# Attention and top-1 routing in one kernel: expert 2's w1 issued behind expert 0's late rows, some routing steps moved in slots 31 to 35, and expert 1's w2 cast by VectorE

## The chip, the cores and the metric

The kernel runs on one core of a Trainium2 chip. The metric is the device time of one execution, in microseconds (us). The time before is 264.27 us, the median of three executions (263.95, 264.27, 265.75). Each kernel also has one profiled execution, from which all the views below come.

## What is computed

The first half is a linear attention for 8 batches of 8 heads, with 576 tokens and 64 channels a head, followed by a norm over each head's channels. The second half takes the result as 4608 tokens of 512 channels, sends each token to one of 8 experts, and runs a two-layer network there.

```python
kv  = einsum('bhsd,bhse->bhde', k, v)
out = einsum('bhsd,bhde->bhse', q, kv)
x   = out / sqrt(mean(out*out, -1) + 1e-6) * g_norm      # then (4608, 512)

logits = x @ w_gate                                       # (4608, 8)
e      = argmax(logits); gate = softmax(logits)[e]
y[mask of expert e] = gate * (relu(xe @ w1[e]) @ w2[e])   # w1: 512x1024, w2: 1024x512
```

## The kernel before

**Attention in 36 slots.** Each of the 36 slots makes 128 rows of x. In slot s PE multiplies the transposed q with the batch's kv (`x_mm`, L334) into a PSUM tile, ACT squares it and VectorE (DVE) adds the squares up (`x_norm`, L348, lines 361 and 365), ACT takes a logarithm and an exponential for the inverse norm, and DVE writes the small logits (L373) and the scaled rows in f16 (L381). PE also transposes the q of two slots ahead (`x_qt`), and ACT copies it out of PSUM (`x_qs`). From slot 31 on the scaling of a slot is held over into the next one.

**Routing.** A `Route` (L396) treats a group of two to five slots: sum the logits, take their maximum (`top`), subtract it (`below`, which gives dl), mark the first maximum (`code`, `first`, `choose`), count with a scan (`tally`), exponentials (`expo`, L467, on ACT), ranks within each expert by three small matmuls of PE (`ranks`, L457, which write into spare columns of a slot's PSUM tile), then the row numbers (`mask`, `send`) and the running total (`total`), all on DVE. `scatter` (L488) is an indirect DMA of GpSimd that writes 128 rows of x, sorted by expert, into a scratch tensor in DRAM (`xs_scratch`). The last three groups are slots 27 to 30, 31 to 33, and 34 to 35.

**Order by hand.** The order on every engine's queue is that of the program text. The slot loop runs lists of closures: `mid` after `x_mm` of the slot, `pre`, `head`, `late` and `last` after it. `at(where, s, fn)` puts a step into one of them, and the table `plan` (L907) gives each group's slots. [...]

**Weights.** A weight matrix is loaded in f32 (2 MB) into one of five staging buffers that it shares with q, k and v (`load_next`, L196: w1 and w2 of expert 0, then of expert 1, and so on), and cast to f16: w1 by DVE (`cast1`, L177) or ACT (`cast1_act`, L183), w2 by ACT (`cast2`, L188), or by DVE where an engine is named (L190).

**Experts.** `fetch` (L664) is a transposing DMA on SP of an expert's rows out of the scratch tensor into xt, with the marks mt (token numbers and gates) in a DMA of their own. It must wait until the scatters in question have landed. The first 384 rows of expert 0 (NE = 3 tiles) and 256 of expert 1 (NA = 2 tiles) are fetched after slot 30, the late rest when the last scatters have landed. `early_one`, `early_pair`, `ahead_pair` and `late_pair` are the first layer on these parts (tiles hpe, hpa, hpl), with a ReLU on ACT into xh; `two` (L782) is the second layer of 128 rows (ype, yp), DVE scales the result (L805) and GpSimd writes it to the output by an indirect DMA (L808).

**After the slots** the text of L1073 to L1137 interleaves the two last groups' routing with the first matmuls of experts 0 and 1; the loop of L1143 then runs the experts: `one` (first layer, four PSUM buffers hp), the casts of the next expert's w1, the loads of w2 three experts ahead and the rows of that expert, `two` for each tile with the casts of the next expert's w2 between them on ACT, and the next w1.

Of the kernel before, what the change touches and what calls it, by code (L numbers as in the profile page):

```python
# [21 lines left out]
def _bc(ap: bass.AP, insert_pos: int, count: int) -> bass.AP:  # L22
    dims = [list(d) for d in ap.ap]
    dims.insert(insert_pos, [0, count])
    return bass.AP(tensor=ap.tensor, offset=ap.offset, ap=dims)
# [3 lines left out]
def kernel(  # L29
# [11 lines left out]
    nc = tc.nc  # L41
# [150 lines left out]
    W = [Weights(e, e) for e in range(E)]  # L192
# [3 lines left out]
    def load_next(count=1):  # L196
        nonlocal n_loads
        for _ in range(count):
            if n_loads < len(loads):
                n, m = loads[n_loads]  # L200
                (W[n].load1 if m == 1 else W[n].load2)(stg[n_loads % 5], nc.sync)
                n_loads += 1
# [93 lines left out]
    def split(s):  # L296
        P, r = divmod(s, 9)
        b = 2 * P + (r >= 4)
        return P, r, b
# [34 lines left out]
    def x_mm(s):  # L334
        P, r, b = split(s)
        if r < 8:
            parts = [(slice(0, 128), kvs_bufs[b % 4])]
        else:
            parts = [(HALF[tok], kvs_bufs[(2 * P + tok) % 4]) for tok in range(2)]
        ops[s] = quad("kvp" if s in (32, 35) else "op", "op")  # L340
        for i4 in range(4):
            for cols, kvs in parts:
                nc.tensor.matmul(  # L343
                    ops[s][cols, i4, 0:144], qts[s][:, i4, cols], kvs[:, i4, :],
                    start=True, stop=True,
                )

    def x_norm(s):  # L348
        P, r, b = split(s)
        if r == 0:  # L350
            xgs[P] = xh[P % 2][:, 0:9 * RW].rearrange("p (g c) -> p g c", g=9)
            lrs[P] = PW.tile([128, 9, 8, 8], F32, tag="lr", bufs=2, name="lr")
        if r == (2, 2, 2, 3)[P]:
            nc.gpsimd.tensor_copy(
                xgs[P][:, :, 512:514].bitcast(I32).rearrange("p g o -> p (g o)"),
                tokc[:, 9 * P:9 * P + 9],
            )
        xg, lr = xgs[P], lrs[P]
        oc = ops[s]
        sq = PW.tile([128, 8, 64], F32, tag="sq", bufs=1, name="sq")  # L360
        nc.scalar.activation(  # L361
            sq.rearrange("p (c i) n -> p c (i n)", i=2), oc[:, :, 0:128], ACTF.Square
        )
        ms = PW.tile([128, 8], F32, tag="ms", bufs=3, name="ms")
        nc.vector.reduce_sum(ms, sq, axis=AXX)  # L365

        def scale():
            lnt = PW.tile([128, 8], F32, tag="lnt", bufs=3, name="lnt")
            nc.scalar.activation(lnt, ms, ACTF.Ln, scale=1.0 / 64.0, bias=epsb)
            rinv = PW.tile([128, 8], F32, tag="rinv", bufs=3, name="rinv")  # L370
            nc.scalar.activation(rinv, lnt, ACTF.Exp, scale=-0.5)  # L371
            r2 = rinv.rearrange("p (c i) -> p c i", i=2)
            nc.vector.tensor_tensor(  # L373
                lr[:, r, :, :].rearrange("p (c i) n -> p c i n", i=2),
                oc[:, :, 128:144].rearrange("p c (i n) -> p c i n", i=2),
                _bc(r2, 3, 8), op=ALU.mult,
            )
            return r2

        def rows(r2):  # L380
            nc.vector.tensor_tensor(  # L381
                xg[:, r, 0:512].rearrange("p (i c n) -> p c i n", i=2, c=4),
                oc[:, :, 0:128].rearrange("p c (i n) -> p c i n", i=2),
                _bc(r2, 3, 64), op=ALU.mult,
            )

        def rest():
            r2 = scale()
            return lambda: rows(r2)

        return rest
# [473 lines left out]
    with tc.tile_pool(name="psattn", bufs=1, space=bass.MemoryType.PSUM) as PSA:  # L865
        first_slot = [9 * (b // 2) + 4 * (b % 2) for b in range(B)]
        mid, pre, head, late, last = ({s: [] for s in range(-4, 40)} for _ in range(5))
# [15 lines left out]
        def at(where, s, fn, *args):  # L883
            where[s].append(lambda: fn(*args))

        for b in range(1, B):
# [24 lines left out]
            ((1, 5, 4), (18, 19, 20, 21), (22, 23, 24, 25)),  # L911
            ((2, 0, 5), (23, 24, 25, 26), (26, 27, 28, 28, 29)),
            ((2, 5, 4), (27, 28, 28, 29), (29, 29, 30, 30)),
            ((3, 0, 4), (31, 31, 31, 32), (32, 33, 33, 34)),
        ]
        for g, (s_sum, s_below, s_oh, s_rank), s_scat in plan:
            rt, G = Route(*g), g[2]
            at(late, s_sum, rt.logits, 0, G)
            at(late, s_below - (s_below == s_oh > s_sum), rt.top)
            at(late, s_below, rt.below)  # L920
            at(late, s_below, rt.code)
            at(late, s_oh, rt.expo)
            at(late, s_oh, rt.first)
            at(late, s_oh, rt.choose)
            at(late, s_oh, rt.tally)
            at(late if s_rank == 32 else mid, s_rank, rt.ranks, s_rank)
            at(late, s_rank, rt.mask)
            at(late, s_rank, rt.send)
            at(late, s_rank + (g[0] < 2), rt.total)
            for t, slot in enumerate(s_scat):  # L930
                at(late, slot, rt.scatter, t, t + 1)
        at(last, 2, load_all, ("k", 4), ("v", 4))
# [10 lines left out]
        at(late, 30, lambda: early_close(ecp[0]))  # L943
        at(last, 30, jobs[0].fetch, 0, NE)
        at(last, 30, jobs[1].fetch, 0, NA)
        at(last, 32, load_next, 1)
        for m in range(8):
            at(last if m < 4 else late, 27 + m, W[0].cast1_act, m)
        for n in range(31, 35):
# [1 line left out]
        rt = Route(3, 4, 3)  # L951
        at(late, 34, rt.logits, 0, 3)
        at(late, 34, rt.top)
        at(late, 34, rt.below)
        at(late, 34, rt.expo)
        at(late, 34, rt.code)
        at(late, 34, rt.first)
        at(late, 34, rt.choose)
# [115 lines left out]
        job.hidden()  # L1074
        x_mm(35)
        rest = x_norm(35)
        relu = [job.early_one(0, "qtp"), job.early_one(1, "misc")]
        rt.ranks(34)
        rt.mask()
# [40 lines left out]
            if t < 2:  # L1120
                W[1].cast1(2 * t)
        jobs[1].fetch(NA, CT)
        load_next(1)
        jobs[2].fetch()
        load_next(1)
        jobs[1].hidden()
# [1 line left out]
        for n, tag in enumerate(tags):  # L1128
            jobs[1].ahead_pair(2 * n, tag)
        jobs[1].place(0, NA, evalid[:, NE:NE + NA], ebig[:, NE:NE + NA])  # L1130
        for m in range(2):
            W[1].cast2(m)
        for n, tag in enumerate(tags):
            job.late_pair(2 * n, tag)
        for m in range(2, 4):
            W[1].cast2(m)
        job.place(NE, CT)  # L1137

    PSF = ctx.enter_context(
# [89 lines left out]
```

## Time and profile before

| | us |
|---|---|
| median of three executions | 264.27 |
| profiled execution | 263.74 |
| span in its profile | 261.9 |
| PE busy | 240.9 (92%) |
| ACT busy | 155.1 (59%) |
| DVE busy | 141.8 (54%) |
| GpSimd busy | 101.7 (39%) |

The span is the time from the first to the last instruction in the profile; the profiled execution's own time has 1.8 us around it. In the profile, PE is TensorE's matmuls, PEld its weight loads, POOL GpSimd, and a name such as SPq is an engine's instruction queue. An entry like `hp<-xt,w1b` names the tile written and the tiles read. The page also gives the DMA totals: 83.13 MB were moved, 317 GB/s in the mean over the span, and 16 weight matrices of 2048 KB were loaded with a median of 13.3 us from issue to landing. The slots run to about 117 us, the interleaved part to about 136, the expert loop to 257.

### The profile page before, as it was taken

How to read it: one execution, taken by the hardware profiler on the slowest of the kernel's cores; microseconds unless marked ns; L12 is line 12 of the kernel's file. 1: busy time of each engine (PE TensorE's matmuls, PEld its weight loads, DVE VectorE, ACT ScalarE, POOL GpSimd, SP SyncE). 2: the span in 40 equal slices, each digit the busy share in tenths (PEclk: the TensorE clock that was granted, in tenths of full speed). 3: DMA queues.
4: the chain of work that ended last, by engine and by line, in shares of the span. 5: the costliest groups of instructions: out<-in, count | busy, mean ns of one | idle time of the engine just before them, and what ended most of it. 6: DMA issues, size and time to landing. Idle time of an engine off the chain costs nothing. (4 is left out here: it accounts for less than half of the span.)

```text
span 261.9 us, 7015 instructions
## 1 busy us (share of the span) xinstructions
PE 240.9 (92%) x2786; PEld 173.2 (66%) x2786; DVE 141.8 (54%) x378; ACT 155.1 (59%) x352; POOL 101.7 (39%) x131
## 2 busy tenths in 40 slices
PE   6899978989999997688989999999999999999991
PEld 6778857878879887564566466475674755746640
DVE  0105566868787787869706860488344255156041
ACT  1056747577677779678595738377375547814600
POOL 4032222776278367455602150521504215034063
PEclk9589999999999999989999999999999999999998
DMA  7999999999999999689599996999999999995023
GB/s 227 386 392 390 392 409 382 395 396 394 392 387 404 410 409 398 263 174 371 167 272 327 392 364 118 317 413 239 353 417 216 390 336 295 350 336 216 1 88 120
DMA packets 52106, 83.13 MB, mean 317 GB/s; under 512 B 27862, under 2 KB 27990, under 8 KB 51944
## 3 DMA queue, kind: packets, MB, share of 16 engines
q1 hardware_dynamic: 46900, 68.28, 77.6%
q0 software_dynamic: 4848, 14.20, 14.4%
q10 hardware_dynamic: 324, 0.19, 0.6%
q8 instruction: 22, 0.36, 0.6%
q14 instruction: 12, 0.10, 0.1%
HBM read 63.42 MB, written 16.17 MB: 304 GB/s over the span
## 5 line engine op out<-in xcount | busy, mean ns | idle before, releaser
L808 POOL DMA_INDIRECT out_dram<-ys,idx x41 | 40.4, 985 | 92.3 <-DVE ys L805 84.3
L743 ACT ACTIVATE xh<-hp 128x304 f16<-128x304 f32 (+2 forms) x104 | 44.9, 431 | 38.2 <-PE hp L731 26.2
L797 PE MATMUL yp<-w2b,xh 128*128 128x512 f16 (+1 forms) x296 | 65.4, 379 | 1.2 <-ACT xh L778 1.2
L731 PEld LDWEIGHTS <-w1b 128*128 128x128 f16 x512 | 49.9, 98 | 19.6 <-issue 1.7
L797 PEld LDWEIGHTS <-xh 128*128 128x128 f16 (+1 forms) x320 | 32.5, 102 | 36.3 <-issue 1.2
L731 PE MATMUL hp<-xt,w1b 128*128 128x304 f16 (+2 forms) x416 | 56.4, 296 | 0.0
L805 DVE TENSOR_SCALAR ys<-yp,gate 128x512 f32<-128x512 f32 (+2 forms) x38 | 27.9, 739 | 50.8 <-PE yp L797 50.8
L343 PE MATMUL op<-kvs,qts 128*128 128x144 f32 (+1 forms) x320 | 44.9, 299 | 0.6 <-ACT kvs L291 0.6
L491 POOL DMA_INDIRECT xs_scratch<-xh,sli x36 | 35.5, 987 | 24.2 <-issue 9.5
L343 PEld LDWEIGHTS op<-kvs,qts 128*128 128x128 f32 (+1 forms) x320 | 37.9, 182 | 3.9 <-issue 0.9
L365 DVE TENSOR_REDUCE ms<-sq 128x8 f32<-128x512 f32 x36 | 24.6, 684 | 21.0 <-ACT sq L361 20.3
L310 POOL COPY qp<-land 128x512 f32<-128x512 f32 x32 | 19.5, 616 | 36.1 <-DMA land<-in_q_dram 25.6
L361 ACT ACTIVATE sq<-op 128x512 f32<-128x512 f32 x36 | 21.4, 595 | 14.8 <-PE op L343 11.1
L188 ACT CAST w2b<-land 128x1024 f16<-128x1024 f32 x26 | 25.5, 1045 | 7.1 <-DMA land<-in_moe_w_dram 7.1
L252 PE MATMUL kvp<-land 64*64 64x64 f32 x1152 | 25.6, 234 | 2.7 <-DMA land<-in_v_dram 2.0
L252 PEld LDWEIGHTS kvp<-land 64*64 64x64 f32 x1152 | 21.4, 143 | 7.5 <-issue 7.0
L320 PE MATMUL qtp<-ident,qp 128*128 128x128 f32 x144 | 22.9, 280 | 2.6 <-issue 2.5
L177 DVE TENSOR_SCALAR w1b<-land,g 128x1024 f16<-128x1024 f32 x26 | 18.0, 749 | 12.5 <-DMA land<-in_moe_w_dram 12.5
L381 DVE TENSOR_TENSOR xh<-op,rinv 128x512 f16<-128x512 f32 x36 | 24.5, 679 | 0.3 <-PE op L465 0.3
L326 ACT COPY qts<-qtp 128x512 f32<-128x512 f32 x36 | 21.0, 583 | 4.0 <-PE qtp L320 3.9
L320 PEld LDWEIGHTS qtp<-ident,qp 128*128 128x128 f32 x144 | 17.0, 143 | 3.4 <-issue 3.2
L373 DVE TENSOR_TENSOR lr<-op,rinv 128x64 f32<-128x64 f32 x36 | 7.9, 220 | 12.7 <-ACT rinv L371 9.9
(134 smaller groups left out, 172.9 us busy)
## 6 DMA issues: line engine op xcount, KB each, us to landing
land<-in_moe_w_dram SPq DMA_DIRECT2D x16, 2048.0 KB, 13.3
land<-in_q_dram SPq DMA_DIRECT2D x8, 1152.0 KB, 15.0
land<-in_k_dram SPq DMA_DIRECT2D x7, 1152.0 KB, 15.9
land<-in_v_dram SPq DMA_DIRECT2D x7, 1152.0 KB, 18.9
land<-in_k_dram SPq DMA_DIRECT2D x2, 576.0 KB, 7.2
land<-in_v_dram SPq DMA_DIRECT2D x2, 576.0 KB, 6.3
xs_scratch<-c_zero SPq DMA_DIRECT2D x1, 774.0 KB
out_dram<-ys,idx POOLq DMA_INDIRECT x41, 6.8
```

Source lines behind the costliest of these rows:

```text
L188: nc.scalar.copy(self.w2[:, part, :], self.s2[:, part, :])
L252: nc.tensor.matmul(kvst[b][HALF[ipar], hh, Dh * ip:Dh * ip + Dh], kb[HALF[hh], i, cols], vb[HALF[hh], i, cols], start=(j == 0), stop=(j == 8),
L320: nc.tensor.transpose(qtps[s][:, ip, :, tok, :], qps[s][:, tok, 2 * ip:2 * ip + 2, :], ident)
L343: nc.tensor.matmul(ops[s][cols, i4, 0:144], qts[s][:, i4, cols], kvs[:, i4, :], start=True, stop=True,)
L365: nc.vector.reduce_sum(ms, sq, axis=AXX)
L381: nc.vector.tensor_tensor(xg[:, r, 0:512].rearrange("p (i c n) -> p c i n", i=2, c=4), oc[:, :, 0:128].rearrange("p c (i n) -> p c i n", i=2),
L491: go = nc.gpsimd.indirect_dma_start(out=xs_views[9 * self.P + g0 + t], out_offset=IndirectOffsetOnAxis(ap=self.sli[:, t:t + 1], axis=0), i ...
L731: nc.tensor.matmul(hp, self.w.w1[:, 2 * (kk % 2) + kk // 2, f // 2 * 256:f // 2 * 256 + 256] .rearrange("p (m r) -> p r m", r=2)[:, f % 2, :],
L743: nc.scalar.activation(self.ht[:, f, c0:c1], hp, ACTF.Relu)
L797: nc.tensor.matmul(yp[0:m, :], self.ht[:, f, t * 128:t * 128 + m], self.w.w2[:, f, :], start=(f == 0), stop=(f == 7),)
L805: nc.vector.tensor_scalar(ys[0:m, 0:d], yp[0:m, 0:d], self.gate[0:m, t:t + 1], None, op0=ALU.mult)
L808: nc.gpsimd.indirect_dma_start(out=view, out_offset=IndirectOffsetOnAxis(ap=self.idx[0:m, t:t + 1], axis=0), in_=ys[0:m, 0:d], in_offset=None,
```

## The change

The change has four parts; the number of loads, scatters, casts and matmuls stays the same.

1. The group of slots 27 to 30 has its exponent one slot later (32 instead of 31), and its ranks, mask, row numbers and total move from the end of slot 32 to slot 33, just after that slot's products. The ranks still use slot 32's PSUM tile. All four of its scatters stand in slot 33 (before: one in 32, two in 33, one in 34).
2. The group of slots 31 to 33 has its exponent after slot 35's norm instead of in slot 34.
3. The load of expert 2's w1, which stood at the end of slot 32, is issued after the fetch of the late rows of experts 0 and 1, ahead of expert 2's w2.
4. The four casts of expert 1's w2 are made by DVE, after the first places of expert 1, instead of by ACT in two pairs around the late pairs' ReLUs.

```diff
-            ((3, 0, 4), (31, 31, 31, 32), (32, 33, 33, 34)),
+            ((3, 0, 4), (31, 31, 31, 33), (33, 33, 33, 33)),
...
-            at(late, s_oh, rt.expo)
+            at(late, s_oh + (s_rank == 33), rt.expo)
...
-            at(late if s_rank == 32 else mid, s_rank, rt.ranks, s_rank)
-            at(late, s_rank, rt.mask)
-            at(late, s_rank, rt.send)
-            at(late, s_rank + (g[0] < 2), rt.total)
+            then = mid if s_rank == 33 else late
+            at(mid, s_rank, rt.ranks, min(s_rank, 32))
+            at(then, s_rank, rt.mask)
+            at(then, s_rank, rt.send)
+            at(then, s_rank + (g[0] < 2), rt.total)
...
-        at(last, 32, load_next, 1)
...
-        at(late, 34, rt.expo)
...
         x_mm(35)
         rest = x_norm(35)
+        rt.expo()
...
         jobs[1].fetch(NA, CT)
-        load_next(1)
+        load_next(2)
         jobs[2].fetch()
         load_next(1)
...
-        for m in range(2):
-            W[1].cast2(m)
+        for m in range(4):
+            W[1].cast2(m, nc.vector)
         for n, tag in enumerate(tags):
             job.late_pair(2 * n, tag)
-        for m in range(2, 4):
-            W[1].cast2(m)
         job.place(NE, CT)
```

## The prediction

> **What bounds the kernel now.** I first read the shares of busy time on the page: PE is busy 92% of the span, so the question is where it still waits. The timeline of PE from 100 to 262 us has only three gaps over 0.5 us after slot 31:
>
> ```profile
> 109.06 0.18 PE L461 MATMUL op<-csum,ones 128*128 128x32 f16 x1 [1.97 <-ACT sq L361]
> 116.53 1.46 PE L731 MATMUL hpe<-xt,w1b 128*128 128x384 f16 x8 [0.72 <-DMA xt<-xs_scratch]
> 136.56 3.61 PE L797 MATMUL yp<-w2b,xh 128*128 128x512 f16 x16 [1.25 <-ACT xh L778]
> ```
>
> The square brackets give the idle time before a piece and what ended it. From 136.56 to the last matmul at 256.5 PE never stops: any shift of PE before that goes to the end, unless something else comes late first. What could come late is seen in the timelines of ACT and DVE over the expert loop:
>
> ```profile
> 180.30 3.88 ACT L188 CAST w2b<-land 128x1024 f16<-128x1024 f32 x4 [1.09 <-DMA land<-in_moe_w_dram]
> 198.66 3.88 ACT L188 CAST w2b<-land 128x1024 f16<-128x1024 f32 x4 [2.48 <-DMA land<-in_moe_w_dram]
> 216.59 3.89 ACT L188 CAST w2b<-land 128x1024 f16<-128x1024 f32 x4 [3.52 <-DMA land<-in_moe_w_dram]
> 221.80 8.18 ACT L743 ACTIVATE xh<-hp 128x304 f16<-128x304 f32 x16 [1.32 <-PE hp L731]
> ...
> 190.99 2.74 DVE L177 TENSOR_SCALAR w1b<-land,g 128x1024 f16<-128x1024 f32 x4 [2.45 <-DMA land<-in_moe_w_dram]
> 209.91 2.74 DVE L177 TENSOR_SCALAR w1b<-land,g 128x1024 f16<-128x1024 f32 x4 [4.48 <-DMA land<-in_moe_w_dram]
> 227.89 2.74 DVE L177 TENSOR_SCALAR w1b<-land,g 128x1024 f16<-128x1024 f32 x4 [5.55 <-DMA land<-in_moe_w_dram]
> ```
>
> The reader is to see that the casts wait for their weights, and wait longer with every expert. PE takes 16.9 us an expert (starts of the hp groups: 204.12, 221.02); the loads need some 18 (below). The stock of loaded weights shrinks by about a microsecond an expert, and the last cast of expert 6's w2 ends at 220.48, only 1.32 us before ACT's first ReLU of that expert. The DMA queue is a second bound, just under PE.
>
> Its own order is in the timeline of SP (start, time at the queue, issue):
>
> ```profile
> 115.60 0.42 SPq L165 DMA_DIRECT2D land<-in_moe_w_dram  x1
> 127.68 1.25 SPq L675 DMA_TRANSPOSE xt<-xs_scratch  x1
> ...
> 132.09 0.82 SPq L171 DMA_DIRECT2D land<-in_moe_w_dram  x1
> ...
> 164.48 16.05 SPq L675 DMA_TRANSPOSE xt<-xs_scratch  x1
> 180.77 0.39 SPq L165 DMA_DIRECT2D land<-in_moe_w_dram  x1
> ...
> 200.94 15.81 SPq L675 DMA_TRANSPOSE xt<-xs_scratch  x1
> 216.99 0.39 SPq L165 DMA_DIRECT2D land<-in_moe_w_dram  x1
> ```
>
> 115.60 is expert 2's w1, 132.09 its w2. From there each expert's transposing load holds SP for 16 us behind the two weight loads, and the next weights are issued at once when it ends: issues at 180.77, 199.01, 216.99 are 18.1 us apart. The stages show the same:
>
> ```profile
> 110.00:112.00 2.00, 2.00 (x11) 1.84 (x11) 1.12 (x6) 1.34 (x4) 0.35 (x1) 0.54 0.04 14
> 122.00:124.00 2.00, 2.00 (x14) 1.12 (x13) 1.91 (x7) 2.00 (x3) 1.52 (x2) 1.00 1.04 427
> 126.00:128.00 2.00, 2.00 (x11) 0.88 (x9) 2.00 (x4) 0.72 (x2) 1.14 (x1) 1.00 0.19 66
> 136.00:138.00 2.00, 1.44 (x7) 0.68 (x7) 0.00 (x0) 2.00 (x4) 0.00 (x0) 1.00 1.00 389
> ```
>
> The last three columns are granted PE clock, DMA share and GB/s. DMA is full at 122 to 124 with expert 2's w1, nearly empty at 126 to 128, and full from 130 to 238 but for some 2.5 us at 161 to 164.
>
> [...] The trace agrees: after the 1.97 us gap the granted clock was 0.5 from 110.25 to 113.66. It also shows that a gap of 1.25 us, at 135.3, brings no dip[...]. [...] SP agrees: at 115.60 it has issued the next load, and then nothing for 12 us, until expert 0's late rows may be read (127.68). So a load placed behind that one cannot use the empty queue ahead of it. [...]
>
> **The change, part by part.**
>
> *Ranks, masks and the first exponent (slots 31 to 33).* ACT waits 1.37 us at 107.69 with the exponent for DVE's dl; behind it are a cast (0.70) and the square of slot 32 (108.44 to 109.01), on which PE's ranks wait: the 1.97 us gap. With the exponent a slot later the square ends near 107.4, and with the ranks after slot 33's products PE has 1.8 us of work (zeros 0.6, products 1.2) until the tally (done at 108.72). The gap goes, and with it the dip: the four pieces from 109.58 to 114.08 took 1.54, 1.06, 1.06, 1.62 where warm ones take 1.14, 0.63, 0.59, 1.14, some 1.5 us. DVE does the same eight operations in another place. The four scatters start at about 110.7 instead of 111.64, back to back on Pool (1.26 apart) as before. PE ends slot 35's products at about 113.3 instead of 115.81.
>
> But next stands the wait for xt. Its load was issued at 111.31, when the scatter of slot 30 (106.22 on Pool) had landed behind expert 1's w2; nothing of that is moved. So it lands at about 116.4 still and PE waits 3.1 us instead of 0.72. **The gain of 2.5 us is lost there.** What remains is that DVE and ACT are ahead: the waits of 0.17, 0.32 and 0.35 us behind xt, with the later exponent moved off ACT ahead of slot 35's square (0.80 us idle at 116.72), shorten xt-to-`two` from 6.76 to about 6.1 us. Ends: -0.7 us if PE stays warm. If the 3.1 us gap makes a cold window, the next 3.41 us of PE work do half: +1.7 at most, of which waits that remained hide some, I take +1.2, net +0.5. [...] So f, the shift of PE and of the last scatters, is **+0.5 (three in four) or -0.7**.
>
> *Expert 1's w2 on DVE.* ACT loses four casts of 1.04; the two between the ReLUs (132.78 to 134.76) delay the last ReLU to 136.51. Without them the last pair's ReLU follows its matmuls (135.32) by 0.6: the gap shrinks from 1.25 to about 0.6, **-0.6 us**. DVE pays 4 x 0.68 = 2.7 us (the row of L190), in a stretch where it idles from 129.7 to 133.4 and from 133.9 to 138.5: nothing. If that cover is gone, expert 0's last places are late, with 4 us to spare.
>
> *Expert 2's w1 behind the late rows.* 2.1 MB at 410 GB/s are 5.1 us. Before, they lie in 117 to 124, where nothing urgent competes (the late scatters wait for DVE and PE, and the last lands 2.6 us after issue). After, they stand on SP ahead of 132.09, behind the wait of 127.68 + f, in a queue that is then full to the end. Every later load moves by **5.1 + f**. The one hole, at 161 to 164, absorbs nothing: it is SP's four register loads between expert 3's rows and expert 4's weights, and moves along. Who is late:
> - expert 2's w1 lands near 140 for a cast at 145.4, its rows near 148 for 153.4: in time.
> - expert 4's w2: casts end 184.18 + 5.1 + f; ReLUs wait for ACT, PE runs on for the four hp buffers, so PE is late by (cast end - PE start - 1.55): 189.28 - 187.22 - 1.55 = +0.5 + f. (1.55 = four blocks of 0.53 less the first ReLU, 0.56.)
> - expert 5: 207.64 - 204.12 - 1.55 = +2.0 + f. Its rows land at 200.9 + 5.1: +1.9 + f.
> - expert 6: 225.58 - 221.02 - 1.55 = **+3.0 + f**. Its rows (SP done 216.75, about 2.1 to landing): the same, +2.9 + f.
> - expert 7: rows 232.45 + 5.1 = 237.55 against 237.92 + 3.0: in time; w2 on DVE has 4 us.
>
> These waits share one cause, so the largest counts, and it takes up PE's other gains: they only lengthen its wait.
>
> **Sum.** 3.0 + f = +3.5 with the cold window, +2.3 without. The profiled execution took 263.74 us (span 261.9 and 1.8 around it): 267.2. It is the lowest of the four known; against the median of 264.27 the sum gives 267.8. I say 267.5.
>
> **Rivals.**
> - *Faster: the load is hidden.* The point is how far the weights come later: up to about 2.1 us (5.1 less the 3.0 at expert 6) PE does not feel it. If the queue catches up, as through fewer collisions with scatters, PE keeps -0.7 - 0.6 = -1.3: 262.4 to 263.0, or -0.1 with a cold window, about 264. For it: the 46% share of DMA from 124 to 130. Against: that hole lies before SP's wait.
> - *Warm front.* +2.3: 266.0 to 266.6. Same mechanism, luckier window.
> - *More cold windows.* The new waits at experts 4 to 6 are 1.1, 1.5 and 1.0 us[...]. PE then brings a further 1.7 us into expert 6, of which 0.7 shows: 268.0 to 268.5, and 269.7 if the third does too. Against: 1.25 us did not.
> - *The moves don't do what they say*, the gap at 109 staying (the tile of slot 32 still held by its square): f = 0, 266.7 to 267.3. Hard to tell in the time; the trace tells it.
>
> **How the numbers follow.** Forecast with cold front 0.40 and with the gap at 109 left 0.05; warm front 0.22; more cold windows 0.13; hidden and fast 0.12, hidden and even 0.08. About 1% (2.6 us) is what this measurement can tell from none. Over 266.9 lie most of the first two, a quarter of the warm ones and all of the fourth: 0.54. Over 1% faster (under 261.6) needs all gains of the first rival and more: 0.06. Range 263.6 to 269.2: it leaves out the fast rival and two repeated cold windows. The likeliest's own range is 266.5 to 268.3.
>
> **What would show it.** In the profile after: no gap at slot 32, slots 33 and 34 warm; a wait of about 3 us for xt near 113 to 116; DMA nearly empty from 117 to 128; expert 2's w1 issued near 131; L188's wait for expert 6's w2 about 8 us; a PE wait on ACT's ReLU in each of the last experts. Wrong, if xt lands before 115, if SP's issue of expert 7's w1 is not near 222, or if the ReLUs of expert 6 don't wait behind the casts.

## The result, and the profile after

The changed kernel takes **266.25 us** in the median (264.31 to 268.09) against 264.02 for the kernel before (262.90 to 265.78) on the same chip: a ratio of 1.0066, 95% interval 1.0045 to 1.0088, or 1.7 us (1.2 to 2.3; the medians lie 2.2 apart). It is slower, as forecast, by about half of the 3.2 us forecast (two thirds by the medians); 266.25 lies inside the stated range. Here and below, ratios leave out executions more than 1.5% above the fastest of the same kernel, and medians keep them.

Its profiled execution took 264.75 us (span 262.9), 1.5 us less than the median, so one of the better ones. A second profile of the same kernel, at 266.55 us, follows with the experiments, and is nearer to its median. First the timeline of PE of the changed kernel, the lines that answer to the three gaps shown before (start, us, engine, line, operation, and in brackets the idle time and what ended it):

```profile
115.41 1.46 PE L731 MATMUL hpe<-xt,w1b 128*128 128x384 f16 x8 [0.90 <-DMA xt<-xs_scratch]
...
131.25 3.24 PE L731 MATMUL hpl<-xt,w1b 128*128 128x224 f16 x32 [0.51 <-DMA xt<-xs_scratch]
135.12 3.61 PE L797 MATMUL yp<-w2b,xh 128*128 128x512 f16 x16 [0.63 <-ACT xh L778]
...
186.25 8.43 PE L731 MATMUL hp<-xt,w1b 128*128 128x304 f16 x64 [0.31 <-DMA xt<-xs_scratch]
203.85 8.43 PE L731 MATMUL hp<-xt,w1b 128*128 128x304 f16 x64 [0.54 <-DMA xt<-xs_scratch]
222.00 8.43 PE L731 MATMUL hp<-xt,w1b 128*128 128x304 f16 x64 [1.09 <-DMA xt<-xs_scratch]
```

The 1.97 us gap of slot 32 is gone, the gap in front of yp has halved (1.25 to 0.63), and PE reaches that point at 135.12, 1.44 us earlier than before. But three waits stand where there was none, ahead of experts 4, 5 and 6, for their rows: 1.94 us together. A fourth, of 0.51, is for expert 0's late rows. Then the timelines of ACT and DVE, the last expert's casts with a wait:

```profile
217.68 3.88 ACT L188 CAST w2b<-land 128x1024 f16<-128x1024 f32 x4 [4.88 <-DMA land<-in_moe_w_dram]
222.77 8.17 ACT L743 ACTIVATE xh<-hp 128x304 f16<-128x304 f32 x16 [1.21 <-PE hp L731]
...
228.83 2.74 DVE L177 TENSOR_SCALAR w1b<-land,g 128x1024 f16<-128x1024 f32 x4 [6.76 <-DMA land<-in_moe_w_dram]
```

All casts wait longer for their weights than before (4.88 against 3.52, 6.76 against 5.55), yet ACT's ReLUs still wait for PE, not PE for them. The timeline of SP gives the queue:

```profile
111.63 1.58 SPq L675 DMA_TRANSPOSE xt<-xs_scratch  x1
...
126.23 1.27 SPq L675 DMA_TRANSPOSE xt<-xs_scratch  x1
...
130.65 0.66 SPq L165 DMA_DIRECT2D land<-in_moe_w_dram  x1
...
168.24 0.42 SPq L165 DMA_DIRECT2D land<-in_moe_w_dram  x1
...
183.25 0.38 SPq L165 DMA_DIRECT2D land<-in_moe_w_dram  x1
...
200.75 0.40 SPq L165 DMA_DIRECT2D land<-in_moe_w_dram  x1
...
218.08 0.39 SPq L165 DMA_DIRECT2D land<-in_moe_w_dram  x1
```

Expert 2's w1 is issued at 130.65, behind the late fetch (126.23). The four last lines are w1 of experts 4 to 7. Counted from each kernel's own late fetch (the transposing load of expert 0's late rows; 127.68 before), they come 42.0, 57.0, 74.5 and 91.9 us after it, before 35.0, 53.1, 71.3 and 89.3: later by 7.0, 3.9, 3.2 and 2.5. So the moved load at first costs the queue more than the 5.1 us reckoned, 7.0, and by expert 7 it has made good 4.5 of them, 3.1 between experts 4 and 5. The view of stages shows where. First the kernel before, then the changed one (stretch; us; busy time of PE, PEld, DVE, ACT and POOL; then granted clock, DMA share, GB/s):

```profile
161.00:164.00 3.00, 3.00 (x18) 1.58 (x17) 0.39 (x1) 2.81 (x5) 0.00 (x0) 1.00 0.21 21
164.00:182.00 18.00, 18.00 (x111) 10.87 (x109) 13.32 (x37) 10.57 (x21) 4.86 (x5) 1.00 1.06 337
```

```profile
165.00:169.50 4.50, 4.50 (x24) 2.43 (x23) 1.93 (x3) 3.49 (x4) 2.87 (x3) 1.00 0.80 249
169.50:184.50 15.00, 15.00 (x96) 9.20 (x94) 12.05 (x36) 8.45 (x18) 3.64 (x4) 1.00 1.04 355
```

Before, the hole that SP's register loads leave in the queue (161 to 164) lay ahead of expert 2's output scatters, which then ran against the next weights: POOL has none in the hole and five behind it. After, the hole has moved into the scatters (three of POOL's in 165 to 169.5) and moves 249 GB/s instead of 21. The next stretch to the following weights is 15 us long instead of 18.1.

### The profile page after: what moved, and what is told of

It is laid out like the page before. It is cut to its first block, busy times and chain, and to the rows that moved or that the text cites. A ratio compares the mean times of both kernels' runs of the same rounds, so it can differ in the third digit from the quotient of the medians.

```text
span 262.9 us, 7015 instructions
## 1 busy us (share of the span) xinstructions
PE 239.8 (91%) x2786; PEld 171.7 (65%) x2786; DVE 144.2 (55%) x382; ACT 151.9 (58%) x348; POOL 101.9 (39%) x131
## 5 line engine op out<-in xcount | busy, mean ns | idle before, releaser
L188 ACT CAST w2b<-land 128x1024 f16<-128x1024 f32 x22 | 21.5, 1042 | 21.2 <-DMA land<-in_moe_w_dram 21.2
L252 PE MATMUL kvp<-land 64*64 64x64 f32 x1152 | 24.7, 226 | 3.8 <-DMA land<-in_v_dram 2.1
L252 PEld LDWEIGHTS kvp<-land 64*64 64x64 f32 x1152 | 20.5, 137 | 8.6 <-issue 8.0
```

The costliest lines, as they stand in the source:

```text
L188: nc.scalar.copy(self.w2[:, part, :], self.s2[:, part, :])
L252: nc.tensor.matmul(kvst[b][HALF[ipar], hh, Dh * ip:Dh * ip + Dh], kb[HALF[hh], i, cols], vb[HALF[hh], i, cols], start=(j == 0), stop=(j == 8),
```

## Experiments

My theory after the result: the loss is the queue's time for the moved load, less what the hole takes back; the front (all that runs up to the second layer of expert 0's late rows) gains in the slots but loses most of it to the wait for expert 0's early rows and the half clock after it. The rivals: the loss comes from the front itself; or from the casts; or the front's gain is lost to something else. The runs fall into four comparisons, each on one chip, with medians of the kernel before of 264.02 (above), 265.13, 267.77 and 264.07 us; ratios are always to the kernel before on the same chip, and gains and losses in us are worked out from them unless medians are named.

**The parts one by one** (second comparison, 265.13). The load alone:

```diff
-        at(last, 32, load_next, 1)
...
         jobs[1].fetch(NA, CT)
-        load_next(1)
+        load_next(2)
```

> The kernel before with one part of the change: expert 2's w1 is issued behind the fetch of the late rows. Theory (the SP queue and DMA set the end; every later load comes later, less what the queue catches up in its idle stretch near 161 to 164 us, now filled with output scatters): slower than before by 2.0 to 3.5 us, PE waiting for xt or for ReLUs in the last experts. Rival (the time lies in the front: the routing moves make PE wait for xt and then run at half clock): within 0.6 us of before.

Measured: 266.46, ratio 1.0051 (1.0028 to 1.0074), 1.35 us slower. Less than the theory's 2.0 to 3.5, more than the rival's 0.6. The timeline of PE has the waits for rows without any routing step moved:

```profile
205.01 8.43 PE L731 MATMUL hp<-xt,w1b 128*128 128x304 f16 x64 [0.34 <-DMA xt<-xs_scratch]
223.22 8.43 PE L731 MATMUL hp<-xt,w1b 128*128 128x304 f16 x64 [1.15 <-DMA xt<-xs_scratch]
```

w1 of experts 4 to 7 comes 5.6, 3.4, 2.4 and 1.9 us later after the late fetch than before: again most of it is given back, with the hole at 164 to 169.5 filled to a DMA share of 0.88.

All but the load, which is the changed kernel with the load put back:

```diff
+        at(last, 32, load_next, 1)
...
-        load_next(2)
+        load_next(1)
```

> The changed kernel with the load of expert 2's w1 put back at the end of slot 32. Theory: faster than before by 1.3 to 2.8 us, since the front and the ReLU wait are gained and no weight comes later; no PE wait in experts 2 to 7. Rival (front): no better than before, 0 to 1.5 us slower, with a clock of 0.5 in a stretch after the wait for xt.

Measured: 265.48, ratio 1.0009 (0.9986 to 1.0031), no different from before. The rival's expectation held here, not mine: PE waits 3.68 us for the early rows and then has a half-clock window (two groups of eight matmuls at 4.30 us, at 2.99 with the clock full); behind 135.94 PE waits for nothing.

The routing steps alone (casts put back on ACT as well):

```diff
+        for m in range(2):
+            W[1].cast2(m)
         for n, tag in enumerate(tags):
             job.late_pair(2 * n, tag)
+        for m in range(2, 4):
+            W[1].cast2(m)
```

> The kernel before with the routing steps and scatters moved in slots 31 to 35, load and casts as before. Theory: faster by 0.7 to 2.2 us, the 1.97 us gap of slot 32 and its cold window gone, the wait for xt at most 3 us. Rival (front): 0 to 1.5 us slower.

Measured: 265.64, ratio 1.0029 (1.0004 to 1.0054): no gain, rather a loss. This profile has only 0.87 us at the early rows, but another wait later on:

```profile
133.22 3.24 PE L731 MATMUL hpl<-xt,w1b 128*128 128x224 f16 x32 [2.38 <-DMA xt<-xs_scratch]
```

The last scatter was issued at 123.52 and the late fetch only at 127.91, 4.4 us later, where the changed kernel needs 2.8 (123.40 to 126.23). In this kernel expert 2's w1 (115.93) was still being loaded; in the changed one that stretch of the queue is free. That is one profile, and the kernel with all but the load needed 2.8 us too (124.31 to 127.10), so the collision is possible, not regular.

The casts alone:

```diff
-        for m in range(2):
-            W[1].cast2(m)
+        for m in range(4):
+            W[1].cast2(m, nc.vector)
         for n, tag in enumerate(tags):
             job.late_pair(2 * n, tag)
-        for m in range(2, 4):
-            W[1].cast2(m)
```

> The kernel before with only expert 1's w2 cast by VectorE. Theory: faster by 0.6 us (PE's gap before the second layer of expert 0's late rows 0.6 instead of 1.25 us). Rival: no change, or up to 0.5 us slower, if the casts hold up VectorE's places or gates.

Measured: 265.02, ratio 0.9991 (0.9969 to 1.0013). The gap is 0.63 in its profile; the 0.6 us can't be told from nothing in the time.

**The load left out** (third comparison, 267.77). Expert 2's w1 is not loaded; the kernel casts what the buffer holds.

```diff
+                if (n, m) == (2, 1):
+                    W[n].s1 = stg[n_loads % 5].rearrange("p (t f) -> p t f", t=4)
+                else:
+                    (W[n].load1 if m == 1 else W[n].load2)(stg[n_loads % 5], nc.sync)
```

> The kernel before with the load of expert 2's w1 left out altogether (2 MB; expert 2 then works on what the buffer holds, so its outputs are not the reference's). Theory (the loss with the load alone is only the queue's time): no PE wait from 135 us on, expert 7's w1 issued 2 us or more earlier than with the load at its late place, time within 0.6 us of before or up to 0.5 us below it. Rival (the loss comes from the place in SP's order or from changed timing in the front): the loss of about 1.3 us stays.

Measured: 267.58, ratio 0.9996 (0.9964 to 1.0027). The loss is gone with the 2 MB, with the rest as in the kernel before. Two details missed: PE waited 2.06 us for the late rows at 137.30 (from 141.18 on for nothing), and expert 7's w1 came 90.1 us after the late fetch, 1.1 us sooner than with the load at its late place, not 2.

**Is the early fetch set by the queue?** The early fetch, of expert 0's first rows, had been issued at 111.3 to 112.3 in six profiles, though slot 31 began anywhere from 101.9 to 104.7. So I took expert 1's w2 out of its way, in the kernel with all but the load:

```diff
-        at(last, 29, load_next, 1)
...
-        at(last, 32, load_next, 1)
+        at(last, 32, load_next, 2)
```

> The changed kernel with expert 2's w1 back at slot 32, and expert 1's w2 also issued there, behind the early fetch (before: at slot 29, ahead of it). In six profiles the early fetch was issued at 111.3 to 112.3 us whatever the time of the slots, as if the DMA queue, full with expert 1's w2 until about 109, set it. Theory (the queue sets the early fetch, and so the routing moves gain nothing): the fetch is issued by 109.5 and the rows land by 113.5, PE waits for them less than 1 us, and the time falls 1 to 2 us below the same kernel without this edit. Rival (the slots set the fetch, the gain is lost elsewhere): issue not before 111, no gain; or the two loads meet the late scatters, and the late fetch comes later than 127.5.

Measured, in the third comparison: 271.26, ratio 1.0131 (1.0074 to 1.0187), clearly slower. The lines are of the timelines of POOL, SP and PE, and of one stage:

```profile
110.79 0.96 POOL L491 DMA_INDIRECT xs_scratch<-xh,sli  x1 [0.30 <-issue]
...
115.45 1.40 SPq L675 DMA_TRANSPOSE xt<-xs_scratch  x1
...
121.28 2.18 PE L731 MATMUL hpe<-xt,w1b 128*128 128x384 f16 x8 [3.03 <-DMA xt<-xs_scratch]
```

```profile
104.00:108.00 4.00, 2.59 (x33) 2.12 (x31) 2.31 (x8) 3.86 (x11) 1.33 (x2) 1.00 0.21 76
```

The queue was nearly empty from 104 on, and the fetch still came 4.7 us after slot 30's last scatter. **The theory is not borne out, but it does not fall either.** The slots ran late in this profile (slot 31 from 107.9). In the trace of the kernel before, the completion events, which the views leave out, show what released SP: the last of that scatter's 16 completions, at 111.19, 0.1 us ahead of the fetch; with expert 1's w2 in the queue they are spread from 108.81 on. What made it 4.7 us here I did not find out. Over all profiles the fetch follows the scatter by 4.0 to 6.4 us but for one (3.0). The second half of the rival came true: the two loads met the late scatters, and the late fetch was issued at 136.30, 6.3 us after the last of them (130.03).

**Half clock in front of expert 0** (third comparison). Where PE waits for the early rows, eight matmuls on zeros are put in:

```diff
         rt.expo()
+        zeros(8)
         relu = [job.early_one(0, "qtp"), job.early_one(1, "misc")]
```

> The changed kernel with expert 2's w1 back at slot 32, and eight matmuls on zeros (1.7 us of PE) put in where PE waits for expert 0's early rows. Theory (half-clock windows after that wait eat the gain): cold time per run falls by about half a window of 3.4 us, and the median by 0.4 to 1.0 us. Rival (the rows themselves set everything behind): less than 0.3 us either way.

Measured: 267.18, ratio 0.9983 (0.9958 to 1.0007). The interval includes no change, and the same kernel without the zeros was not run on this chip. Its profile has a shorter wait and no slow matmul behind it:

```profile
116.67 1.90 PE L876 MATMUL warm<-blank 128*128 128x512 f16 x8
120.15 1.46 PE L731 MATMUL hpe<-xt,w1b 128*128 128x384 f16 x8 [1.58 <-DMA xt<-xs_scratch]
...
121.53 2.99 PE L731 MATMUL hpe<-xt,w1b 128*128 128x384 f16 x16
```

**The hole taken out** (third comparison). Expert 3's rows are fetched after SP's register loads instead of ahead of them:

```diff
-            if n + 4 < E:
+            if 0 < n and n + 4 < E:
                 jobs[n + 3].fetch()
...
                     W[e].e = jobs[e].row = bass.ds(ev, 1)
+                jobs[3].fetch()
```

> The changed kernel with expert 3's rows and marks fetched after SP's four register loads instead of ahead of them, so that expert 4's weights follow without the 3 us in between. Theory (the end is set by the load queue, and its idle stretch near 165 to 169 us still holds about 1 us): PE's waits for xt in experts 4 to 6 (1.9 us in the profile) shrink by 0.9 to 1.9 us, and the time by as much. Rival (PE or the front sets the time): no change within 0.4 us.

Measured: 268.25, ratio 1.0024 (0.9995 to 1.0052). The changed kernel itself was not run on that chip, so this alone decides nothing.

**Side by side** (fourth comparison, 264.07). The changed kernel again:

> The changed kernel once more, on the same chip as the three that follow. Theory (load queue at the end, front worth nothing in the mean): slower than before by 1.2 to 2.3 us, PE waiting for xt in experts 4 to 6 by 0.3 to 1.5 us each.

Measured: 265.75, ratio 1.0044 (1.0018 to 1.0070), 1.2 us slower (1.7 in the medians), at the low end of what was expected. The timeline of PE shows the wait that the prediction spoke of, and two stages the clock:

```profile
116.85 2.72 PE L731 MATMUL hpe<-xt,w1b 128*128 128x384 f16 x8 [3.46 <-DMA xt<-xs_scratch]
```

```profile
113.30:116.85 3.55, 0.09 (x2) 0.10 (x1) 2.59 (x9) 1.73 (x6) 2.28 (x3) 0.95 1.09 225
117.30:120.60 3.30, 3.30 (x17) 1.69 (x15) 0.88 (x6) 1.43 (x3) 0.16 (x1) 0.61 0.18 47
```

PE is idle for 3.46 us, and in the stage behind the wait its granted clock is 0.61: the eight matmuls take 2.72 instead of 1.46. It then waits 0.46, 0.17 and 1.17 us for the rows of experts 4 to 6. Next to it the kernel without the hole:

> The changed kernel with expert 3's rows fetched after SP's register loads, to stand beside the changed kernel on the same chip. Theory (the queue's remaining idle stretch is worth about 1 us): 0.7 to 1.6 us faster than the changed kernel. Rival (PE or front): within 0.4 us of it.

Measured: 264.97, ratio 1.0012 (0.9987 to 1.0037), 0.8 us below the changed kernel in the medians. The intervals overlap, so the times alone don't show that it is faster; the timeline of SP shows the edit at work:

```profile
148.71 0.49 SPq L165 DMA_DIRECT2D land<-in_moe_w_dram  x1
149.31 1.22 SPq L171 DMA_DIRECT2D land<-in_moe_w_dram  x1
...
154.66 11.10 SPq L675 DMA_TRANSPOSE xt<-xs_scratch  x1
165.97 0.41 SPq L165 DMA_DIRECT2D land<-in_moe_w_dram  x1
```

Expert 4's w1 follows the end of the rows' issue (165.76) at once, 37.9 us after the late fetch instead of 41.4, though by expert 7's w1 only 0.5 us of the 3.5 is left: the step from expert 4's w1 to expert 5's is 18.2 us again. Over all profiles that step takes 15.0 to 15.9 us where the load is late and the hole is there, and 17.8 to 19.2 in all others, which speaks for the hole and the scatters as what gave the 3 us back. The waits at experts 4 to 6 fall from 1.80 to 1.25 us. Then all but the load:

> The changed kernel with expert 2's w1 back at slot 32, on the same chip. Theory: 1.1 to 2.0 us faster than the changed kernel, within 0.6 us of the kernel before, no PE wait for xt after 135 us. Rival (the load at its late place spares the late scatters and is worth as much as it costs): no faster than the changed kernel.

Measured: 263.96, ratio 0.9997 (0.9967 to 1.0027), 1.8 us below the changed kernel in the medians (1.2 by the ratios) and equal to the one before, as expected. Its profile has 3.61 us at the early rows and a half-clock window behind (a granted clock of 0.55 from 116.8 to 120.1). With zeros in that wait:

> The kernel of the last row with eight matmuls on zeros in PE's wait for expert 0's early rows, on the same chip. Theory (cold windows behind that wait eat the front's gain): 0.4 to 1.0 us faster than without them, with less cold time a run; so below the kernel before. Rival (the rows' arrival sets all): within 0.3 us of it.

Measured: **263.01, ratio 0.9957 (0.9934 to 0.9979)**: faster than the kernel before by 1.1 us and the best of all. It is 0.95 us below the kernel without the zeros in the medians (0.2 to 1.9, by resampling both). The clock records of the traces before and after show 1.0 and 0.5 alone. So, as an estimate from the granted clock and span of each execution, cold time in the mean is twice the missing clock times the span: 7.8 us without the zeros, 6.2 with them, 6.9 before. Half of the 1.6 us, 0.8, would account for most of the gain. But the 1.6 us can't be told from nothing (-0.4 to 3.7), and the changed kernel, with its wait unfilled, has 6.1 us of cold time on this chip. So the gain is measured; that it comes from the clock is likely, not shown. The profile, of an execution 3 us above the median, has a wait for the late rows in place of the early one, and half clock behind it (4.90 us for what takes 3.24 elsewhere):

```profile
133.34 4.90 PE L731 MATMUL hpl<-xt,w1b 128*128 128x224 f16 x32 [2.29 <-DMA xt<-xs_scratch]
```

## Why the prediction was right, and which term was too large

**Direction: right. Mechanism: right for the rows, wrong for the casts.** The load put behind the late fetch makes every later load late, and PE waits for it in experts 4 to 6. Leaving the 2 MB out brings the loss to zero; the load alone costs 1.35 us (0.7 to 2.0), and everything but the load 0.2 and -0.1 us in two comparisons. Whether gains ahead would only lengthen PE's wait, as was said, no run shows, since in the mean there were none. Of the three signs named for being wrong two came: expert 7's w1 was issued at 218.08 (219.77 in the second profile), not near 222, and expert 6's ReLUs did not wait behind the casts; L188's wait for expert 6's w2 was 4.88 us, not about 8.

**The term that was mis-sized is the load's 3.0 us.** The step was "The one hole, at 161 to 164, absorbs nothing: it is SP's four register loads ..., and moves along." It does move along, but the output scatters do not move with it: they keep to PE's time, and the hole, come later, falls on them. A queue's idle stretch was taken for lost because SP's order makes it, without asking what other traffic would then fall into it. The rival "hidden" had the idea ("fewer collisions with scatters") but was looked for in the wrong hole, that of 124 to 130. Further ground, 1 to 2 us, is made good between experts 5 and 7 in all profiles with the late load; I did not trace its cause.

**A misreading the other way made up for part of it, which is luck.** The 2.1 us from SP to landing were taken over from expert 5's rows. By the completion events in the trace before, expert 6's rows took 3.2 and landed at 219.97, not 218.85, so that PE had 1.05 us to spare there and not 2.2. With that, the full 5.1 us would have given 4.0 and not 2.9. What came, counted from the late fetch, were rows 2.8 us later with the load alone, and 3.4 and 2.7 in the changed kernel's two profiles. As an estimate, the load's term is 2.8 - 1.05, or 1.7 us, against the 1.35 measured; each figure is from one profile, and in profiles without the late load SP is done with these rows from 1.0 us earlier to 0.5 later than in the one before (89.07 us after the late fetch).

**Which wait would be last: half right.** Casts of w2 with the ReLUs behind them (+3.0) and rows (+2.9) were given as equal; it was the rows alone. In the changed kernel the last cast of expert 6's w2 ended at 221.56, and its rows held PE until 222.00.

**The front: right in size, one reason open.** Said: PE finishes slot 35 about 2.5 us sooner, the gain is lost at the early rows with a wait of 3.1 us, and a half-clock window follows (three in four, odds of mine that no run showed). Seen in four profiles with the routing moved: waits of 3.45 to 3.68, each with the window; in three (the changed kernel's first, the routing alone and the first without the hole): 0.74 to 0.90, without. From the rows to the second layer it is 6.35 us warm (said: 6.1) and 7.45 cold in the changed kernel's two profiles (said: 7.3). Together with the casts the front was to give -0.1 or -1.3 us; 0.2 and -0.1 were measured. That expert 1's w2 in the queue sets the time of the early fetch is neither shown nor refuted. What I had not reckoned with is a further wait for the late rows, 0.4 to 3.0 us in nine profiles; three of these have the routing of before, so the moved routing is not its only cause.

**The casts on DVE: right in the trace** (gap of 0.63 against 0.6), not to be told in the time.

**The likeliest case and the range.** 267.5 was the likeliest and 266.25 came; the warm front's 266.0 to 266.6 held the median, but for another reason, a smaller load term; that it fell there is luck. The forecast gave most of the weight to over 1%; it was 0.7%.

## What to carry to other kernels

Before moving a load to a later place on a queue that waits as this one did (SP issued nothing from 116.02 to 127.68 before the change), follow the queue to the end of the kernel: with the queue nearly as long as PE's work, free time given up ahead of a wait came back behind it only in part (2.5 of 7.0 us were still missing at expert 7). When traffic is shifted, ask for every idle stretch of the queue what other traffic will then meet it; traffic that keeps to another engine's time may fill it (here 249 GB/s instead of 21). And a PE gap that is closed in front of an arrival that stays only moves to the arrival (1.97 us went, and 3.45 to 3.68 stood at the early rows in four profiles): there, matmuls on zeros in the wait were worth more (0.95 us) than all the steps that closed the gap (-0.2 and 0.1).

## What the runs showed of the hardware that I had not expected

- A wait of PE of 3.5 us cost more than itself (the changed kernel's second profile): matmuls of 1.46 us took 2.72 afterwards, at a granted clock of 0.61 in that stage. Before the change 1.97 us were enough (0.50 from 110.17 to 113.59), and in the changed kernel's first profile 0.90 us were not (1.46 behind them). But the length of the gap alone does not tell: 2.06, 2.38 and 2.96 us ahead of the late rows (the load left out, the routing alone, expert 1's w2 moved) left 3.24 us behind them, where 2.29 in the kernel with the zeros brought 4.90.
- In the clock records the half-clock stretches begin at 7.77, 110.17 and 260.36 before and at 35.77 and 261.05 after, a multiple of 3.41 us apart within each trace. PE's idle time in the 3.41 us ahead of the three that begin before the end of its work was 2.02, 1.97 and 1.88 us. 1.25 us (134.07 to 137.48 before) and 1.46 us (5.05 to 8.46 after) were followed by full clock. These are two traces; what decides is not shown.
- From the issue of slot 30's scatter, the last of four, to the load that depends on it, 4.0 to 6.4 us passed in all profiles but one (3.0), with the queue nearly empty (a DMA share of 0.21 from 104 to 108) 4.7; for the last scatter of the late group 2.6 to 3.0 in most profiles (up to 6.3).
- Four register loads on SP take 3.1 us before the change (3.4 to 3.7 where scatters run beside them) and leave the load queue nearly empty for some 2.5 us there (a DMA share of 0.21 from 161 to 164).
- Executions of one kernel on one chip differ by 3 to 4 us (264.31 to 268.09), several times what most parts of this change are worth.
